# A contiguous copy by ScalarE ahead of the forward transform along d, with the planner's costs and order drawn anew

## The chip, the cores and the metric

One core of one Trainium2 chip runs the kernel. The metric is the device time of one execution in microseconds, the median of several runs.

## The reference

x is one sequence of S = 2048 tokens with D = 576 values each. Two branches read it and a gate per token mixes them.

```python
g = _sigmoid((x * gate_w).sum(-1, keepdims=True))
# branch a: a spectral filter over tokens and features
X = jnp.fft.rfft2(x, axes=(-2, -1)) * (w_r + 1j * w_i)
a = jnp.fft.irfft2(X, s=(S, D), axes=(-2, -1))
# branch b: 32 heads, each picks one of 64 x 64 = 4096 experts
q = jnp.einsum("nd,dhc->nhc", xf, w_q)            # 2 x 128 per head
s1 = jnp.einsum("nhd,ed->nhe", q[..., :128], k1)  # 64 scores
s2 = jnp.einsum("nhd,ed->nhe", q[..., 128:], k2)  # 64 scores
e = argmax(s1) * 64 + argmax(s2)
act = _gelu(jnp.einsum("nd,nhkd->nhk", xf, u[e]))
b = jnp.einsum("nhk,nhk,nhkd->nd", softmax(best, over 1), act, v[e])
return g * a + (1 - g) * b
```

All of it is float32. The two argmax lists decide which rows of u and v each token reads.

## The kernel before, in words

**Branch b, scores.** The 2048 tokens are 16 tiles of 128. The heads come in 8 chunks of 4; a chunk has 4 x 2 x 64 = 512 score columns. `build_m` multiplies the chunk's part of w_q with the keys (line 452, "build"), and ScalarE cuts the product into a high and a low part, mh and ml (lines 457 and 464). `scores` (line 472 on) takes a pair of token tiles and multiplies their x, also cut in two parts, with mh and ml: 14 matmuls of 128x512 for a tile and chunk, so 1792 in all. VectorE takes the maximum over each 64 columns (`mx`, line 502), ScalarE the sign of the distance to it (`sg`, line 510), and a few small steps make the index of the row (`ei`).

**Branch b, rows.** For each token tile and each head one gather (GpSimd, line 636 or 743) brings 128 rows of u and v side by side, 128 x 2 x 576 floats = 590 KB, into one of 12 buffers `uv` (13 in the late part). There are 512 gathers. VectorE forms the dot product with x (line 648, or 752 in the late part), ScalarE the gelu (line 652 or 755), and the factor `a` follows (line 657, 661 or 756). The v half is added up in one of three ways: by VectorE, by ScalarE and VectorE together, or by TensorE as a matmul with a diagonal matrix `dg` (made in line 702, used in line 706). The tiles 0 to 10 go through `group`. The tiles 11 to 15 go through `quad`, which works on four heads at once in quarters of the partitions; it needs x repeated four times (`xr`, line 733, 16 copies by ScalarE for each tile), a diagonal from VectorE (`dg`, line 758) and eight small matmuls (line 766).

**Branch a.** Its buffers take the place of those of the scores, so it begins when the last scores are done. `fold` (line 890 on) brings each of the 16 token tiles into the tile `BT` of 128 x 5 x 128 x 16 floats: partition, block of features, token group, and phase q of 16. `f2` (line 926) is the forward transform along d for one q: six matmuls (`along`, line 919), each recorded as two passes, that take `BT[:, i, :, q]` as the stationary operand, so 128 columns that lie 16 floats apart. `f4` (line 945), `f5` (line 965) and `f6` (line 975) transform along the tokens, multiply with the weights and go back; the result is written into the same slots of `BT`. `unit_front` calls `f2` for q = k and, but for k = 0 and 8, for q = 8 + k too, 16 calls in all. `invert` (line 1066 on) goes back along d: also `along`, with 128 columns of `BT` that lie side by side, and a second product (`go9`). The mix and the store follow.

**What sets the order.** Nothing is in a fixed order by hand. Every operation is a job with an engine, a duration, a due time and the buffers that it touches. `Plan.order` plays the jobs through: an engine that is free takes the ready job with the earliest due time that gets its buffers. Durations and latencies are numbers in the code (`REACH`, `LAND` and `HOP` in lines 101 to 103, and the second argument of each `plan`, `dv` and `ac`); due times are offsets (lines 1147 to 1192) plus a table `NUDGE` of some 900 entries. Each engine then runs its jobs in the order of that play, in order: an instruction that waits holds up those behind it.

Of the kernel before, what the change touches and what calls it, by code (L numbers as in the profile page):

```python
# [17 lines left out]
ALU = mybir.AluOpType  # L18
AX = mybir.AxisListType

P = 128
# [255 lines left out]
def tile_kernel(ctx, tc, xn, xT, x5, wqT, wq5, kT, wri, uv, gw, t_kr, t_ff, t_fv, t_tw, t_io, out):  # L277
# [162 lines left out]
    def build_m(c, i, at, after=()):  # L440
# [14 lines left out]
        plan("PE", 1.7, at, go, [pm], [wq, kTb], after=after)  # L455
# [16 lines left out]
    def scores(c, tp, at):  # L472
# [7 lines left out]
        def part(j, i):  # L480
# [12 lines left out]
            return plan("PE", 0.2275 * len(seq), at, go, [(ps, j)], list(use.values()))  # L493
# [13 lines left out]
        def signs(j, g0):  # L507
# [5 lines left out]
            plan("ACT", 0.784, at + O_SIGN, go, [sg], [(ps, j), (mv, tp)])  # L513
# [12 lines left out]
        dv(0.07 + 512 / 1920, at + O_MIN + nd("n", c, tp), lambda: vt(sq.ap[:, k], s2()[:, :, : E // 2], s2()[:, :, E // 2 :], ALU.min), [(sq, k)], [sg])  # L526
# [7 lines left out]
        dv(0.07 + n * 256 / 1920, at + O_MIN + nd("n", c, tp), lambda: vt(q2()[:, :, :Q], q2()[:, :, :Q], q2()[:, :, Q:], ALU.min), keys, [])  # L534
        dv(0.07 + n * 256 / 1920, at + O_MIN + nd("n", c, tp), lambda: vt(q2()[:, :, :Q], q2()[:, :, :Q], ramp.ap[:, :Q].unsqueeze(1).to_broadcast([P, n * 4 * HPC, Q]), ALU.add), keys, [ramp])
# [36 lines left out]
    def shuffle(src, dst, c0, c1, at, rd, wr):  # L572

        for q in range(HPC):
# [6 lines left out]
            plan("ACT", 4 * 0.2, at + O_TURN, go, wr, rd)  # L581
# [47 lines left out]
    def group(t, c, at, ahead, gate_by=(), ks=range(HPC), mixed=False):  # L629
# [22 lines left out]
        ac(0.1, at + O_GELU, lambda: actv(b.ap[:, k0:k1], z.ap[:, k0:k1], AF.Gelu_apprx_tanh), [b], zk, table="gelu")  # L652
# [47 lines left out]
        for k in range(0 if t in PAIR else HPC):  # L700
# [8 lines left out]
            plan("PE", 0.97, at + (O_D if t < NE else O_DL) + nd("p", t, c), go, [pd], [dg, (rows[k], 1)])  # L709
# [16 lines left out]
    def repeat(t, at, after):  # L726
# [4 lines left out]
        for j in range(HPC):  # L731
            for q in range(HPC):
                ac(act(576), at + 0.6 * j, lambda j=j, q=q: actv(  # L733
                    xr[t][j].ap[QB * q : QB * q + QB, :], x.ap[QB * j : QB * j + QB, :], AF.Copy), [(xr[t][j], q)], [x], after=after)

    def quad(t, c, at, ahead, gate_by, last):
# [18 lines left out]
        ac(0.1, at + O_QGELU, lambda: actv(b.ap, z.ap, AF.Gelu_apprx_tanh), [b], [(z, j) for j in range(HPC)], table="gelu")  # L755
# [14 lines left out]
        quads[t, c] = plan("PE", 1.25, at + O_QD + nd("p", t, c), go, [pd], [dg] + [(g, 1) for g in rows])  # L770
# [82 lines left out]
    for m, tag, pool, n in (  # L853
            (0, "bt", "la", 1), (0, "f5", "la", 2), (0, "kr", "la", 1), (0, "rp", "la", 1), (0, "eiq", "la", 1), (1, "lq", "lb", 1), (1, "krb", "lb", 1),
# [35 lines left out]
    def fold(t, at):  # L890
# [22 lines left out]
        plan("PE", 2.5, at, go, [pb], [(f, i) for i in range(5)] + [(kr, 0), (kr, 1), (kr, 2)])  # L913
# [31 lines left out]
    def f4(k2, X, at):  # L945
# [16 lines left out]
        plan("PE", 1.95, at, go, [p], [X, (tw, 0), (tw, 1)])  # L962
# [12 lines left out]
    def f6(k2, zb, tw, at):  # L975
# [16 lines left out]
        plan("PE", 2.39, at, go, [pt], [(zb, 0), (zb, 1), (tw, 0), (tw, 2), (tw, 3)])  # L992
# [26 lines left out]
    def unit_back(z, at):  # L1019
# [20 lines left out]
        dv(0.21, at, lambda: vt(BT.ap[:, 2, :, qc], ta.ap[:, 512:], pb.ap[:, 1, :P], ALU.add), [c_], src)  # L1040
        dv(0.21, at, lambda: vt(BT.ap[:64, 2, :, qs], pb.ap[64:, 1, :P], ta.ap[64:, 512:], ALU.subtract), [s_], src)
        dv(0.21, at, lambda: vt(BT.ap[64:, 2, :, qs], ta.ap[:64, 512:], pb.ap[:64, 1, :P], ALU.subtract), [s_], src)
# [23 lines left out]
    def invert(t, at):  # L1066
# [6 lines left out]
        plan("PE", 2.0, at, go, [p], [fv] + every)  # L1073
# [15 lines left out]
        plan("PE", 1.95, at + 3, go9, [p9], [(krb, 0), (krb, 1), (w, 0), (w, 1)])  # L1089
# [59 lines left out]
O_LESS = -173.264  # L1149
O_S0 = -1609.196  # L1150
A_ACT = True
A_OF = {0: (1, 6), 1: (3, 5, 6), 2: (0, 1, 2, 3, 4, 5, 6), 3: (0, 2, 4, 5, 6), 4: (0, 3, 4, 5, 6), 5: (0, 2, 5, 6, 7), 6: (0, 1, 5, 6), 7: (1, 2, 3, 4, 7), 8: (5, 6), 9: (0, 1, 4, 6, 7), 10: (1, 4, 7), 11: (0, 3, 4, 5, 6), 12: (0, 1, 4, 7), 13: (0, 1, 2, 6), 14: (0, 1, 2, 5, 7), 15: (0, 2, 5)}
O_SCALE = 232.282
# [239 lines left out]
```

## Time and profile before

| | us |
|---|---|
| median of 3 runs | 969.99 (968.39 to 970.98) |
| the profiled execution | 966.69 |
| its span, first to last instruction | 964.9 |
| TensorE busy / weight loads | 895.5 / 711.5 |
| VectorE busy | 835.1 |
| ScalarE busy | 642.9 |
| GpSimd busy | 556.4 |

1.8 us of the profiled execution lie around the span, and it is 3.3 us under the median. PE is TensorE's matmuls, PEld its weight loads, DVE VectorE, ACT ScalarE, POOL GpSimd, SP the queue of plain loads and stores. In the lists of instructions the columns are start, duration (both us), engine, line, operation, out<-in, the shape, and xN for N records; a bracket tells how long the engine stood idle before and who released it. Tile names stand without numbers: `p` is a PSUM tile, `fi` a transform table, `bt` the tile `BT`.

### The profile page before, as it was taken

What the parts mean: (1) busy time and instruction counts of PE and PEld (TensorE: products, weight loads), DVE (VectorE), ACT (ScalarE), POOL (GpSimd) and SP (SyncE); (2) the same over time, 40 slices, a digit from 0 to 9 for tenths busy, and PEclk for the clock granted to TensorE, in tenths of its full rate; (3) what the DMA queues carried; (4) which work ended last, traced back from release to release, by engine and by line L of the source; (5) the groups of instructions that cost most, each with busy time, mean ns of one, the idle gap of its engine ahead of it and who ended that gap; (6) DMA issues with size and microseconds to landing.
All of it is one profiled execution on the core that took longest, in us unless ns stands there. A gap on an engine that the chain in (4) does not pass through costs nothing.

```text
span 964.9 us, 16362 instructions
## 1 busy us (share of the span) xinstructions
PE 895.5 (93%) x5078; PEld 711.5 (74%) x5078; DVE 835.1 (87%) x2026; ACT 642.9 (67%) x2237; POOL 556.4 (58%) x516
## 2 busy tenths in 40 slices
PE   7899999967999999997999999959799999997998
PEld 6788888855888888876878787736467777765775
DVE  3679999989999999998999999859866899886876
ACT  3798977679777767577796989895642431615433
POOL 0227565746666665666656676637766556546661
PEclk9999999988999999998999999979999999998999
DMA  9769999988999999998999999999999999999996
GB/s 327 241 237 356 372 370 384 360 293 302 399 356 349 410 369 334 408 368 326 385 369 374 364 388 366 393 362 349 378 393 365 391 354 398 343 369 362 381 417 242
DMA packets 90902, 345.06 MB, mean 358 GB/s; under 512 B 10112, under 2 KB 10752, under 8 KB 90816
## 3 DMA queue, kind: packets, MB, share of 16 engines
q0 software_dynamic: 73728, 302.02, 82.4%
q1 hardware_dynamic: 17088, 42.01, 11.8%
q8 instruction: 40, 0.66, 0.3%
q14 instruction: 46, 0.38, 0.1%
HBM read 339.27 MB, written 4.72 MB: 356 GB/s over the span
## 4 chain that ended last, share of the span: by engine, by line
PE 53%; DVE 19%; ACT 11%; DMA 10%; issue 4%; POOL 1%; SPq 1%; DVEq 0%; ACTq 0%; POOLq 0%
PE p L346 53%; DVE uv L648 5%; DMA uv<-uv,ei 5%; ACT sg L510 3%; DVE xn L680 3%; ACT xr L733 3%; DVE xn L674 2%; DMA tw<-t_tw 2%; DVE uv L752 2%; DVE mx L502 2%; ACT uv L673 1%; POOL uv L636 1%; DMA xl<-xn 1%; DMA uv<-wqT 1%; DMA uv<-wq 1%
## 5 line engine op out<-in xcount | busy, mean ns | idle before, releaser
L636 POOL DMA_INDIRECT uv<-uv,ei x352 | 386.8, 1099 | 280.7 <-PE p L346 62.8
L648 DVE SCALAR_TENSOR_TENSOR uv<-uv,xn 128x576 f32<-128x576 f32 x352 | 260.4, 752 | 5.8 <-DMA uv<-uv,ei 5.7
L346 PE MATMUL p<-mh,xt 128*128 128x512 f32 x768 | 261.9, 399 | 0.8 <-DVE xn L718 0.8
L510 ACT ACTIVATE sg<-p,mx 128x64 bf16<-128x64 f32 x1024 | 235.1, 375 | 37.6 <-DVE mx L502 32.2
L743 POOL DMA_INDIRECT uv<-uv,eiq x160 | 169.4, 1059 | 108.8 <-PE p L346 55.1
L346 PE MATMUL p<-uv,dg 128*32 128x288 f32 (+1 forms) x1104 | 172.0, 423 | 36.4 <-DVE dg L758 15.9
L346 PE MATMUL p<-ml,xt 128*128 128x512 f32 x448 | 176.6, 394 | 0.0
L346 PEld LDWEIGHTS p<-uv,dg 128*32 128x32 f32 (+1 forms) x1104 | 107.8, 147 | 83.9 <-DVE dg L758 19.2
L346 PEld LDWEIGHTS p<-mh,xt 128*128 128x128 f32 x768 | 144.8, 189 | 33.4 <-DVE xn L718 1.3
L346 PE MATMUL p<-mhx,xt 128*128 128x512 f32 x384 | 136.4, 404 | 7.9 <-ACT sg L510 7.0
L752 DVE SCALAR_TENSOR_TENSOR uv<-uv,xr 128x576 f32<-128x576 f32 x160 | 116.7, 752 | 0.7 <-DMA uv<-uv,eiq 0.5
L346 PEld LDWEIGHTS p<-ml,xt 128*128 128x128 f32 x448 | 84.4, 188 | 17.7
L346 PE MATMUL p<-kT,uv 128*128 128x128 f32 x640 | 80.9, 283 | 15.2 <-ACT sg L510 6.2
L346 PEld LDWEIGHTS p<-kT,uv 128*128 128x128 f32 x640 | 79.3, 198 | 20.1 <-ACT sg L510 6.7
L346 PEld LDWEIGHTS p<-mhx,xt 128*128 128x128 f32 x384 | 73.2, 191 | 24.8 <-ACT sg L510 7.2
L680 DVE SCALAR_TENSOR_TENSOR xn<-uv,a,xn 128x576 f32<-128x576 f32 x111 | 89.6, 810 | 0.2
L674 DVE TENSOR_TENSOR xn<-uv,xn 128x576 f32<-128x576 f32 x114 | 86.0, 755 | 4.2 <-ACT uv L673 3.9
L502 DVE TENSOR_REDUCE mx<-p 128x16 f32<-128x1024 f32 x64 | 77.9, 1219 | 13.2 <-PE p L346 13.1
L673 ACT ACTIVATE uv<-uv,a 128x576 f32<-128x576 f32 x114 | 84.3, 813 | 5.2 <-DVE a L661 5.2
L521 ACT ACTIVATE sg<-sg 128x256 bf16<-128x256 bf16 x192 | 81.5, 470 | 0.7
L346 PE MATMUL p<-fi,bt 128*128 128x145 f32 (+3 forms) x384 | 80.3, 363 | 0.9 <-ACT t L1014 0.9
L346 PEld LDWEIGHTS p<-fi,bt 128*128 128x128 f32 x384 | 71.3, 248 | 8.8 <-issue 3.5
(117 smaller groups left out, 1080.7 us busy)
## 6 DMA issues: line engine op xcount, KB each, us to landing
uv<-wqT SPq DMA_DIRECT2D x32, 512.0 KB, 7.2
uv<-uv,ei POOLq DMA_INDIRECT x352, 6.9
w<-wri SPq DMA_DIRECT2D x16, 289.0 KB, 6.6
out<-xn SPq DMA_DIRECT2D x16, 288.0 KB, 5.9
xn<-xn SPq DMA_DIRECT2D x11, 288.0 KB, 6.1
uv<-uv,eiq POOLq DMA_INDIRECT x160, 7.1
tw<-t_tw SPq DMA_DIRECT2D x9, 256.0 KB, 6.9
uv<-xT SPq DMA_DIRECT2D x8, 256.0 KB, 7.2
```

The source lines that it names most:

```text
L346: after("PE", nc.tensor.matmul(*args, **kw))
L502: dv(dve(1024, True), at + O_MAX + nd("m", c, tp), lambda: nc.vector.tensor_reduce(mv.ap[:, 2 * tp : 2 * tp + 2, :], ps.ap.rearrange("p a ...
L510: on("ACT", actv(sg.ap[:, j, g, :], ps.ap[:, j, g * E : g * E + E], AF.Sign, bias=mv.ap[:, 2 * tp + j, g : g + 1], scale=-1.0))
L521: ac(act(256), at + O_ADD, lambda b=b: actv(s2()[:, :, b * Q : b * Q + Q], s2()[:, :, b * Q : b * Q + Q], AF.Copy, bias=b / 4), [sg], [])
L636: on("POOL", nc.gpsimd.indirect_dma_start(out=g.ap.rearrange("p a d -> p (a d)"), out_offset=None, in_=uv, in_offset=bass.IndirectOffsetOn ...
L648: dv(0.68, at + O_DOT + nd("d", t, c), lambda k=k, g=rows[k], xk=xk: stt(g.ap[:, 0, :], g.ap[:, 0, :], 1.0, xk.ap, op0=ALU.mult, op1=ALU.m ...
L673: ac(act_by(576), at + O_SCALE + nd("v", t, c), lambda v=v, s=s: actv(v(), v(), AF.Copy, scale=s()), [(rows[k], 1)], [a])
L674: dv(dve(576), at + O_SUM + nd("v", t, c), lambda v=v: vt(y.ap, v(), y.ap, ALU.add), [y], [(rows[k], 1)])
L680: dv(0.73, at + O_SUM + nd("v", t, c), lambda v=v, s=s: stt(y.ap, v(), s(), y.ap, op0=ALU.mult, op1=ALU.add), [y], [(rows[k], 1), a])
L733: ac(act(576), at + 0.6 * j, lambda j=j, q=q: actv(xr[t][j].ap[QB * q : QB * q + QB, :], x.ap[QB * j : QB * j + QB, :], AF.Copy), [(xr[t][ ...
L743: on("POOL", nc.gpsimd.indirect_dma_start(out=g.ap.rearrange("p a d -> p (a d)"), out_offset=None, in_=uv, in_offset=bass.IndirectOffsetOn ...
L752: dv(0.68, at + O_QDOT + nd("d", t, c), lambda j=j: stt(rows[j].ap[:, 0, :], rows[j].ap[:, 0, :], 1.0, xr[t][j].ap, op0=ALU.mult, op1=ALU. ...
```

## The change

`f2` gets one more step. ScalarE copies the 5 x 128 columns of one q into a contiguous tile `fl`, and the six matmuls read that. There is one such tile. The planner gets other durations and latencies, new offsets, and a new `NUDGE` table, so nearly every engine's order is another one. No other operation is added, taken away or given to another engine.

```diff
-REACH = {'POOL': 3.72, 'SP': 1.04}
+REACH = {'POOL': 2.7, 'SP': 1.04}
-HOP = {'PE': 0.36, 'DVE': 0.05, 'ACT': 0.32, 'POOL': 0.97, 'SP': 0.23}
+HOP = {'PE': 0.3, 'DVE': 0.12, 'ACT': 0.2, 'POOL': 0.6, 'SP': 0.23}
...
-            return plan("PE", 0.2275 * len(seq), at, go, [(ps, j)], list(use.values()))
+            return plan("PE", 0.236 * len(seq), at, go, [(ps, j)], list(use.values()))
...
-                ac(act(576), at + 0.6 * j, lambda j=j, q=q: actv(
+                ac(0.69, at + 0.6 * j, lambda j=j, q=q: actv(
...
+            (0, "bt", "la", 1), ..., (1, "fl", "lb", 1), (1, "lq", "lb", 1), (1, "krb", "lb", 1),
...
     def f2(q, at):
         p = psum()
-
-        def go():
-            along(p, ff, HO, lambda i: BT.ap[:, i, :, q])
-
-        plan("PE", 2.0, at, go, [p], [ff, (BT, "q", q)] + [(BT, "in", t, i) for t in range(NT) for i in range(3)])
+        flat = buf("fl", [P, ND, P])
+        ac(act(640), at + O_FLAT, lambda: actv(flat.ap, BT.ap[:, :, :, q], AF.Copy), [flat], [(BT, "q", q)] + [(BT, "in", t, i) for t in range(NT) for i in range(3)])
+        plan("PE", 2.0, at, lambda: along(p, ff, HO, lambda i: flat.ap[:, i, :]), [p], [ff, flat])
         return p
...
-        dv(0.21, at, lambda: vt(BT.ap[:, 2, :, qc], ta.ap[:, 512:], pb.ap[:, 1, :P], ALU.add), [c_], src)
+        dv(0.395, at, lambda: vt(BT.ap[:, 2, :, qc], ta.ap[:, 512:], pb.ap[:, 1, :P], ALU.add), [c_], src)
...
-ROWS = 1.5
+ROWS = 1.45
...
-    ('a', 0, 0): 4.95, ('a', 0, 1): -78.87, ('a', 0, 2): 294.57, ('a', 0, 3): 155.15, ('a', 0, 4): 38.86, ('a', 0, 5): -72.04,
...
```

The other durations move in the same manner: a build from 1.7 to 1.74, four signs from 0.784 to 0.81, an inverse transform from 2.0 to 2.06, `f4` from 1.95 to 2.1, a fold from 2.5 to 2.4, a quad's matmuls from 1.25 to 1.14.

**First place: TensorE in the forward transform along d.** Before, two transforms (PSUM tiles 1351 and 1365) stand next to each other and both read `bt`; the rows are the second half of one and the first half of the next.

```order
L346 MATMUL p2_1351_7986<-fi_1271_6732,bt_1269_6932 128x145
L346 MATMUL p2_1351_7986<-fi_1271_6732,bt_1269_6932 128x144
L346 MATMUL p2_1351_7986<-fi_1271_6732,bt_1269_6932 128x289
L346 MATMUL p2_1365_8009<-fi_1271_6732,bt_1269_6932 128x145
L346 MATMUL p2_1365_8009<-fi_1271_6732,bt_1269_6932 128x144
L346 MATMUL p2_1365_8009<-fi_1271_6732,bt_1269_6932 128x289
```

After the change two transforms still stand next to each other, and they read two copies, `fl` 7947 and 8026, that lie in the same buffer one after the other.

```order
L346 MATMUL p_1352_8010<-fi_6668,fl_7947 128x145
L346 MATMUL p_1352_8010<-fi_6668,fl_7947 128x144
L346 MATMUL p_1352_8010<-fi_6668,fl_7947 128x289
L346 MATMUL p_1355_8033<-fi_6668,fl_8026 128x145
L346 MATMUL p_1355_8033<-fi_6668,fl_8026 128x144
L346 MATMUL p_1355_8033<-fi_6668,fl_8026 128x289
```

The order of the two is unchanged; between them there is now a copy on another engine. Of the 16 transforms five follow the one ahead directly, as here; three more have one quad's eight small matmuls between, and the other seven have more.

**The same place on ScalarE, after the change.** Line 929 is the copy; `b` is a gelu of the quads (line 755), `t2` the transform's way out of PSUM, `dg` a diagonal.

```order
L929 ACTIVATE fl_1353_7947<-bt_1269_6762 128x640
L1011 ACTIVATE t2_1375_7950<-p2_1373_7917 128x289
L702 ACTIVATE dg_1141_7953<-ident_81,a_1136_7924 128x128
L1012 ACTIVATE t2_1375_7950<-p2_1373_7917 128x289
L755 ACTIVATE b_1624_7965<-z_1623_7908 128x4
L929 ACTIVATE fl_1356_8026<-bt_1269_6762 128x640
L755 ACTIVATE b_1632_8029<-z_1631_7976 128x4
L929 ACTIVATE fl_1389_8050<-bt_1269_6762 128x640
```

Each copy stands in ScalarE's queue behind the gelus and diagonals of the rows, and a gelu stands behind a copy that needs the buffer of the one ahead.

**Second place: ScalarE where the scores end and branch a begins.** The rows are the copies `xr` of the first late tile, and the way to a diagonal `dg` of an early tile. Before, from the end of the copies:

```order
L733 ACTIVATE xr_1523_6911<-xl_1275_6720 32x576 x4
L616 ACTIVATE lq_1_6756<-lq_1_6756 128x160
L510 ACTIVATE sg_1206_6750<-p2_1205_6583,mx_1061_5915 128x64 x4
L621 ACTIVATE lq_1_6756<-lq_1_6756 128x160
L915 ACTIVATE bt_1269_6932<-p2_1311_6705 128x2x128
L941 ACTIVATE tw_1331_6739<-tw_1331_6739 128x128
L942 ACTIVATE tw_1331_6739<-tw_1331_6739 128x2x128
L943 ACTIVATE tw_1331_6739<-tw_1331_6739 128x128
L652 ACTIVATE b_1262_6939<-z_1261_6836 128x4
L887 ACTIVATE krb_1273_6743<-krb_1273_6743 128x128
L521 ACTIVATE sg_1206_6750<-sg_1206_6750 128x16x16
L657 ACTIVATE a_1263_6943<-b_1262_6939,sw_1062_6542 128x1 x4
```

Behind these stand two more copies of `tw` and then `dg` 1265, the next diagonal that TensorE needs; ahead of them stand seven more `xr` copies in a row. After the change:

```order
L733 ACTIVATE xr_1536_6791<-xl_1275_6655 32x576 x2
L616 ACTIVATE lq_1_6700<-lq_1_6700 128x160
L733 ACTIVATE xr_1536_6791<-xl_1275_6655 32x576
L621 ACTIVATE lq_1_6700<-lq_1_6700 128x160
L733 ACTIVATE xr_1536_6791<-xl_1275_6655 32x576
L733 ACTIVATE xr_1537_6826<-xl_1275_6655 32x576 x4
L733 ACTIVATE xr_1538_6836<-xl_1275_6655 32x576 x3
L652 ACTIVATE b_1238_6846<-z_1237_6719 128x4
L733 ACTIVATE xr_1538_6836<-xl_1275_6655 32x576
L657 ACTIVATE a_1239_6851<-b_1238_6846,sw_1062_6404 128x1 x4
L733 ACTIVATE xr_1539_6857<-xl_1275_6655 32x576
L702 ACTIVATE dg_1241_6861<-ident_81,a_1239_6851 128x128
```

The whole row of sixteen `xr` copies has stretched out: the diagonal of the group that TensorE needs next (`dg` 1241) now follows thirteen of them and no `tw` copy. On TensorE two folds stand right ahead of that group; before, a fold and another group (`dg` 1138 to 1141) stood ahead of `dg` 1265.

More of the change, by code (lines that the diff above doesn't have):

```diff
@@ L768, in go @@
                        start=c == 0, stop=c == NCH - 1)
-        quads[t, c] = plan("PE", 1.25, at + O_QD + nd("p", t, c), go, [pd], [dg] + [(g, 1) for g in rows])
+        quads[t, c] = plan("PE", 1.14, at + O_QD + nd("p", t, c), go, [pd], [dg] + [(g, 1) for g in rows])
         if c < NCH - 1:
@@ L911, in go @@
                            start=n == 0, stop=n == 1)
-        plan("PE", 2.5, at, go, [pb], [(f, i) for i in range(5)] + [(kr, 0), (kr, 1), (kr, 2)])
+        plan("PE", 2.4, at, go, [pb], [(f, i) for i in range(5)] + [(kr, 0), (kr, 1), (kr, 2)])
         for r in range(2):
@@ L1184 @@
 TPS = 12.22
-AHEAD = -114.454
-TLAG = -61.614
+AHEAD = -283.177
+TLAG = 12.546
 FPACE = 1.418
```

61 lines of the change are left out of this document (31 added, 30 removed), and 293 rows, old and new, of the table NUDGE.

## The prediction

> **What bounds the kernel now.** I read the page's sums first, then its slices, then the chain that ended last, then every idle stretch of TensorE.
>
> ```profile
> span 964.9 us, 16362 instructions
> PE 895.5 (93%) x5078; PEld 711.5 (74%) x5078; DVE 835.1 (87%) x2026; ACT 642.9 (67%) x2237; POOL 556.4 (58%) x516
> PEclk9999999988999999998999999979999999998999
> DMA  9769999988999999998999999999999999999996
> GB/s 327 241 237 356 372 370 384 360 293 302 399 356 349 410 369 334 408 368 326 385 369 374 364 388 366 393 362 349 378 393 365 391 354 398 343 369 362 381 417 242
> DMA packets 90902, 345.06 MB, mean 358 GB/s; under 512 B 10112, under 2 KB 10752, under 8 KB 90816
> PE 53%; DVE 19%; ACT 11%; DMA 10%; issue 4%; POOL 1%; SPq 1%; DVEq 0%; ACTq 0%; POOLq 0%
> ```
>
> Three resources are nearly full: TensorE at 93%, VectorE at 87%, the DMA engines at nine tenths in most slices. The chain spends 53% of the span on TensorE. TensorE is idle for 964.9 - 895.5 = 69 us. Six stretches make more than half of it; each row below is the work that follows one, with the idle time in its bracket.
>
> ```profile
> 204.26 6.62 PE L346 MATMUL p<-uv,dg 128*128 128x288 f32 x16 [5.07 <-ACT sg L510]
> 222.61 0.80 PE L346 MATMUL p<-mhx,xt 128*128 128x512 f32 x1 [7.03 <-ACT sg L510]
> 447.00 3.78 PE L346 MATMUL p<-kT,uv 128*128 128x128 f32 x16 [6.24 <-ACT sg L510]
> 645.21 6.32 PE L346 MATMUL p<-uv,dg 128*128 128x288 f32 x16 [11.30 <-ACT dg L702]
> 700.62 2.15 PE L346 MATMUL p<-uv,dg 128*32 128x288 f32 x16 [6.15 <-DVE dg L758]
> 872.43 2.15 PE L346 MATMUL p<-uv,dg 128*32 128x288 f32 x16 [4.16 <-DVE dg L758]
> 232.37 4.15 PE L346 MATMUL p<-uv,dg 128*128 128x288 f32 x16 [0.32 <-ACT sg L510]
> ```
>
> Their sum is 39.95 us, 28.65 without the one at 645. The last row is the same group of sixteen as the first after a short wait: 4.15 us against 6.62, and 6.32 behind the stretch of 11.30. So the work behind a long stretch runs 2.2 to 2.5 us slower, say 2.3, and the digits of the granted clock dip in those slices. A long stall costs its idle time plus 2.3 us; the five without the one at 645 cost 28.65 + 5 x 2.3 = 40.2 us, or 8.0 us each.
>
> **The copy and the transforms.** The two users of `bt` as weights differ only in the step between columns; the first row is the stretch of f2, the second that of `invert`.
>
> ```profile
> L346 PEld LDWEIGHTS p<-fi,bt x192: 291/311/319, 724.5 to 850.1; 128*128 128x128 f32 x192
> L346 PEld LDWEIGHTS p<-fi,bt x175: 186/189/193, 883.8 to 953.1; 128*128 128x128 f32 x175
> 730.73 5.60 PE L346 MATMUL p<-fi,bt 128*128 128x145 f32 x24
> 895.67 4.20 PE L346 MATMUL p<-fi,bt 128*128 128x145 f32 x24
> 724.00:852.00 128.00, 125.08 (x867) 96.46 (x866) 107.46 (x275) 44.42 (x108) 72.69 (x71) 1.00 0.98 372
> ```
>
> The median load takes 311 ns with the step and 189 ns without. Two transforms in a row take 5.60 us with it, two of `invert` 4.20, so a contiguous stationary operand saves (5.60 - 4.20) / 2 = 0.70 us for each f2, **11.2 us** for 16. TensorE is busy for 125.08 of 128 us in that stretch, so this is time of the engine that sets the pace there.
>
> The copy costs ScalarE time and makes TensorE wait. No such copy is in the trace. These rows bound it: a write with the same step against one of runs of 16 side by side, and a plain copy.
>
> ```profile
> L915 ACT ACTIVATE bt<-p x32: 362/374/406, 641.5 to 721.2; 128x256 f32<-128x256 f32 x32
> L1025 ACT ACTIVATE bt<-p x4: 593/600/603, 743.9 to 879.4; 128x256 f32<-128x256 f32 x4
> L733 ACT ACTIVATE xr<-xl 32x576 f32<-32x576 f32 x80 | 54.4, 680 | 1.0
> 846.91 0.41 ACT L1013 ACTIVATE t<-p 128x289 f32<-128x289 f32 x1 [3.24 <-PE p L346]
> 847.22 0.41 ACT L1014 ACTIVATE t<-p 128x289 f32<-128x289 f32 x1
> 847.68 3.09 PE L346 MATMUL p<-fi,bt 128*128 128x145 f32 x12 [0.86 <-ACT t L1014]
> ```
>
> If the step costs ScalarE nothing, 640 elements take 0.680 x 640 / 576 = 0.76 us. If it costs what the weight load pays, (311 - 189) / 128 = 0.95 ns a column, they take 0.76 + 0.61 = 1.37 us; what the write pays is (600 - 374) / 256 = 0.88 ns, nearly the same. The load reads the very same addresses, so I take 1.3 us. ScalarE is busy for 44.42 of those 128 us, and 16 x 1.3 = 21 us find room; in time they aren't free. There is one tile `fl`, so a copy waits until the transform ahead has read it. Five times the next transform follows directly, and there TensorE stands still for the whole round trip. The last three rows show one: ScalarE's two copies last 847.63 - 846.91 = 0.72 us and TensorE's gap is 0.86, so a round trip is the copy plus 0.14 us. That gives 5 x 1.44 = 7.2 us. Three times a quad's matmuls lie between, 1.18 us (row below); they leave 0.3 us uncovered, 0.9 in all. The other seven have `f4`, `f6` or more between, over 2 us, and cost nothing; without that cover each would cost 1.4. In the copy's place 8.1 us come back, and the transforms bring **11.2 - 8.1 = 3.1 us**; with the fast copy (0.90 x 5 = 4.5 back) 6.7.
>
> ```profile
> 880.15 1.18 PE L346 MATMUL p<-uv,dg 128*32 128x288 f32 x16 [1.26 <-DVE dg L758]
> 632.65 7.60 ACT L733 ACTIVATE xr<-xl 32x576 f32<-32x576 f32 x11
> 626.31 2.46 PE L346 MATMUL p<-kr,f 128*128 128x256 f32 x24
> 640.27 0.34 ACT L616 ACTIVATE lq<-lq 128x160 f32<-128x160 f32 x1
> 641.30 0.35 ACT L621 ACTIVATE lq<-lq 128x160 f32<-128x160 f32 x1
> 642.49 0.22 ACT L652 ACTIVATE b<-z 128x4 f32<-128x4 f32 x1
> 643.10 0.85 ACT L657 ACTIVATE a<-b,sw 128x1 f32<-128x1 f32 x4
> 644.77 0.97 ACT L702 ACTIVATE dg<-ident,a 128x128 f32<-128x128 f32 x3
> ```
>
> The Trainium skill, "TensorE: Matmul & The Clock Gate", section "LDWEIGHTS (loading the stationary operand)", gives a weight load a time by its number of columns alone, whatever their step. By that rule f2 would save nothing and the round trips would be pure loss, the third rival below; the two rows of loads, 311 and 189 ns at equal columns, speak against it.
>
> **The place at 645 us.** TensorE waits 11.30 us for a diagonal that ScalarE makes at 644.77, behind eleven `xr` copies (7.60 us), signs and copies of `tw`. In the new order the next diagonal stands behind thirteen `xr` copies, 13 x 0.68 = 8.8 us, and the four small steps of the rows, 0.34 + 0.35 + 0.22 + 0.85 = 1.8 us, from the first copy on; on TensorE two folds of 2.46 us cover 4.9 us of that. What is left is 5.7 us, if the copies begin when the first fold does. So **5.6 us** go. It is still long enough for the slow stretch behind it. VectorE's dots end late there too, which bounds the gain: the stall can also stay whole, or go whole (0 to 11.3).
>
> **The rest of the order.** No engine gets other work, so only waits can change. One row shows that the new durations come nearer to what is recorded: a bt addition is planned at 0.395 us instead of 0.21, and an `xr` copy at 0.69 instead of 0.56 where its row above has 0.680.
>
> ```profile
> L1040 DVE TENSOR_TENSOR bt<-f,p x7: 355/374/375, 765.1 to 868.0; 128x128 f32<-128x128 f32 x7
> DVE uv L648 <- DMA uv<-uv,ei: 5.7, 10, 1.1
> DMA to landing us min/median/max: 4.5/6.9/14.3
> POOL uv L636 <- PE p L346: 62.8, 46, 9.9
> POOL uv L743 <- PE p L346: 55.1, 37, 6.2
> ```
>
> An order laid by better numbers meets fewer surprises, but it is a new order of the same crowded engines and brings stalls of its own. How many of the other five long stalls go isn't in any row: none to five of them bound it on the good side, some more of them on the bad side. I take one net, **8.0 us**, by judgement.
>
> The sum is 3.1 + 5.6 + 8.0 = 16.7 us. Against the profiled execution of 966.69 that is 950.0; it was 3.3 us under the median of 969.99, so I predict **953.3**.
>
> **Rivals.**
>
> More stalls go. If three of the five go, the sum is 3.1 + 5.6 + 24.0 = 32.7 and the time 937.3. For it: PE's 69 idle us and the slow work behind them are the largest loss in the profile. Against it: VectorE and DMA are nearly full as well.
>
> Nothing changes, because the stream of rows is the limit. It moves the same 345.06 MB, and its share is 0.98 in the transforms' stretch. What TensorE saves would come back as waiting for rows, and the time stays 970.0. Against it: seven slices reach 393 to 417 GB/s, at 400 the bytes need 863 us, and GpSimd waits 62.8 + 55.1 us for matmuls to free its buffers, so an earlier matmul also starts a gather earlier. The Trainium skill, "SBUF — State Buffer", section "A bandwidth-pool intuition that's wrong (but worth ruling out)", gives one core about 358 GB/s from HBM, the very mean of the page; by that figure the bytes alone would need an estimated 964 us and this rival would be sure. The slices at 384 to 417 speak against it as a limit here.
>
> The load isn't faster. If the 311 ns come from something other than the step, say from what else runs in that stretch, f2 saves nothing, the round trips stay, and the sum is 8.1 - 5.6 - 8.0 = -5.5: 964.5. Against it: all 192 loads lie between 291 and 319 ns, all 175 others between 186 and 193, with no overlap.
>
> Slower: VectorE waits for rows. The planner's latency of a gather on idle DMA engines, from GpSimd's start to VectorE's, was 1.45 + 3.72 + 1.5 + 0.2 + 0.97 = 7.84 us and becomes 1.45 + 2.7 + 1.45 + 0.2 + 0.6 = 6.40 (the 1.45 of GpSimd and the 0.2 of LAND stay). Landings take 6.9 us in the median. With 7.84 VectorE waited for rows only 5.7 us in the whole span; with 6.40 the plan adds its own queueing to a smaller base, and more dots come up before their rows. VectorE is in order, so the maxima and factors behind such a dot wait too, and with them the signs, the PSUM tiles and TensorE. The price is 8.0 us for each wait that grows long. The 8.7 us of the first two terms are used up by 1.1 more long stalls than before; with three more it is 24.0 - 8.7 = 15.3 us slower, 985.3. Against it: 4.5 us is the shortest landing, so 6.40 isn't too short for a queue that is empty.
>
> **How the numbers follow.** The forecast has a chance of 0.42 (its own range 942 to 965), three stalls gone 0.13, the slow load 0.07, no change 0.10, slower 0.28. Below 967.1 lie the first three: faster by over 0.3% (about what a measurement of this kernel can tell from no change) 0.62; within it 0.10; slower 0.28. The range reaches from below the second case to above the last, 931 to 988; some 0.06 lies under it and 0.10 over it.
>
> **What would show it.** Right: the weight loads from `fl` take about 189 ns; a transform of twelve records about 2.1 us; sixteen copies about 1.3 us each; idle times of TensorE of about 1.4 us before the direct followers, released by the copy; some 5.7 us idle where the scores end; five slow stretches of the clock, not six; PE busy about 11 us less. Wrong: copies of 0.8 us or above 1.5; loads of 311 ns; VectorE waiting for rows by tens of us instead of 5.7; idle times over 4 us at new places.

## The result, and the profile after

The changed kernel takes 973.9 us (median of 20 runs, 970.2 to 976.8) against 967.1 us of the kernel before beside it (20 runs, 965.0 to 971.0). The ratio is 1.0064, with an interval of 1.0050 to 1.0077: 0.6% slower, where 953.3 us, 1.4% faster, was forecast. The profiled execution took 975.08 us.

The page of the changed kernel, the lines that answer to those of before:

```profile
span 973.3 us, 16358 instructions
PE 892.2 (92%) x5078; PEld 697.0 (72%) x5078; DVE 838.9 (86%) x2026; ACT 663.2 (68%) x2253; POOL 567.6 (58%) x516
PEclk9999999999999999999999999979899999998999
DMA  9959989798899998899999999999999999999997
GB/s 328 298 204 360 388 304 386 251 333 313 314 384 354 370 384 323 305 379 356 326 343 382 347 349 347 394 367 361 411 393 410 394 368 410 363 391 378 392 417 304
DMA packets 90902, 345.06 MB, mean 355 GB/s; under 512 B 10112, under 2 KB 10752, under 8 KB 90816
DMA 27%; PE 24%; DVE 21%; issue 12%; POOL 7%; ACT 7%; SPq 0%; POOLq 0%; DVEq 0%; ACTq 0%
```

TensorE has 3.3 us less work (892.2 against 895.5) and 12 us more idle time (973.3 - 892.2 = 81.1 against 69.4). The chain that ended last runs through other engines: TensorE had 53% of it and has 24%, the transfers had 10% and have 27%. The rates show some of the places where transfers were missing: slices 8, 16 and 17 are at 251, 323 and 305 GB/s, where before they were at 360, 334 and 408.

The span in three stretches, cut at the first matmul of the forward transform along d and at the first of the inverse one, first of the kernel before, then of the changed one. The columns are the length, then busy time (and instructions) of PE, PEld, DVE, ACT and POOL, the granted clock, the DMA share and GB/s.

```profile
0.00:724.80 724.80, 669.41 (x3447) 541.15 (x3448) 641.55 (x1523) 555.77 (x2007) 427.13 (x391) 0.97 0.95 356
724.80:881.30 156.50, 147.28 (x1058) 109.65 (x1057) 131.25 (x338) 49.58 (x123) 87.56 (x86) 0.98 0.97 369
881.30:964.90 83.60, 78.81 (x580) 60.65 (x576) 62.31 (x166) 37.55 (x108) 41.76 (x39) 0.99 0.89 349
```

```profile
0.00:732.00 732.00, 673.04 (x3431) 539.78 (x3432) 635.76 (x1501) 552.28 (x1994) 428.13 (x383) 0.98 0.93 345
732.00:888.00 156.00, 138.95 (x1057) 96.15 (x1055) 139.03 (x356) 71.83 (x150) 93.74 (x91) 0.98 1.01 390
888.00:973.30 85.30, 80.24 (x596) 61.05 (x592) 64.15 (x170) 39.13 (x110) 45.75 (x43) 1.00 0.94 367
```

Of the 8.4 us by which the span grew, 7.2 lie ahead of the first forward transform, where one copy of the 16 has run. In the middle stretch TensorE is busy for 8.3 us less (138.95 against 147.28), and the stretch is as long as before: the gain is there, and it has turned into idle time. The DMA share has gone the other way: lower in the first stretch (0.93 against 0.95), higher in the two others (1.01 and 0.94 against 0.97 and 0.89), since nine more of GpSimd's gathers are left when the first stretch ends (91 + 43 against 86 + 39).

The new steps of the changed kernel, its weight loads, its copies, one transform that directly follows another, and the waits that belong to the copy (in us: total, times, longest):

```profile
L346 PEld LDWEIGHTS p<-fi,fl x192: 186/189/193, 731.7 to 860.9; 128*128 128x128 f32 x192
L929 ACT ACTIVATE fl<-bt x16: 1283/1314/1341, 725.4 to 858.0; 128x640 f32<-128x640 f32 x16
760.09 2.23 PE L346 MATMUL p<-fi,fl 128*128 128x145 f32 x12 [1.41 <-ACT fl L929]
PE p L346 <- ACT fl L929: 8.2, 8, 1.5
ACT fl L929 <- PE p L346: 30.6, 14, 7.1
```

The loads take 189 ns, the copies 1.31 us, a transform 2.23 us where it took 2.8, and TensorE waits 8.2 us for copies, eight times. All of that is close to the forecast (189 ns, 1.3 us, 2.1 us, 8.1 us). TensorE's busy time isn't: it was to fall by about 11 us and fell by 3.3, with 3.6 us more ahead of the transforms. The last row isn't in the forecast either: ScalarE stood 30.6 us at copies whose tile `fl` was still being read, and what was behind them in its queue stood too.

TensorE's longest idle times in the changed kernel, after its start:

```profile
229.47 0.79 PE L346 MATMUL p<-mhx,xt 128*128 128x512 f32 x1 [4.55 <-ACT sg L510]
650.23 6.78 PE L346 MATMUL p<-uv,dg 128*128 128x288 f32 x16 [8.77 <-ACT dg L702]
703.41 6.92 PE L346 MATMUL p<-uv,dg 128*128 128x288 f32 x32 [5.54 <-ACT dg L702]
881.63 4.76 PE L346 MATMUL p<-tw,t 128*128 128x256 f32 x24 [2.53 <-DVE t L969]
```

Where there were six of 4.2 to 11.3 us there are three of 4.6 to 8.8, and the digits of the granted clock dip in three slices instead of five. So long stalls did go, and yet TensorE is idle for longer: by many short waits. What grew is this, waits of the changed kernel (the first was 5.7 us in 10 times before):

```profile
DVE uv L648 <- DMA uv<-uv,ei: 47.2, 69, 2.1
DVE uv L752 <- DMA uv<-uv,eiq: 20.2, 34, 1.2
POOL uv L636 <- DVE xn L680: 53.5, 28, 14.8
L636 POOL DMA_INDIRECT uv<-uv,ei x352: 933/1070/2494, 37.1 to 745.6; - x176
DMA to landing us min/median/max: 4.3/6.9/16.1
```

VectorE meets its rows late 103 times, 67 us in all, none of them longer than 2.1 us, and GpSimd waits 53.5 us for buffers that VectorE's sums free late. Of the kernel before, the same wait of GpSimd:

```profile
POOL uv L636 <- DVE xn L680: 10.7, 13, 1.9
```

The median landing of the 352 early gathers is 6.9 us as before; the longest is 16.1 instead of 14.3. That of the 160 late gathers rises from 7.1 to 8.4 us.

### The profile page after: what moved, and what is told of

Same layout as the page of the kernel before. It is cut to its first block, busy times and chain, and to the rows that moved or that the text cites. A ratio compares the mean times of both kernels' runs of the same rounds, so it can differ in the third digit from the quotient of the medians.

```text
span 973.3 us, 16358 instructions
## 1 busy us (share of the span) xinstructions
PE 892.2 (92%) x5078; PEld 697.0 (72%) x5078; DVE 838.9 (86%) x2026; ACT 663.2 (68%) x2253; POOL 567.6 (58%) x516
## 3 DMA queue, kind: packets, MB, share of 16 engines
q0 software_dynamic: 73728, 302.02, 82.2%
q1 hardware_dynamic: 17088, 42.01, 11.8%
## 4 chain that ended last, share of the span: by engine, by line
DMA 27%; PE 24%; DVE 21%; issue 12%; POOL 7%; ACT 7%; SPq 0%; POOLq 0%; DVEq 0%; ACTq 0%
PE p L346 24%; DMA uv<-uv,ei 19%; POOL uv L636 6%; DVE uv L648 6%; DMA uv<-uv,eiq 5%; DVE xn L680 3%; DVE xn L674 3%; ACT sg L510 2%; DVE mx L502 2%; DMA xl<-xn 2%; ACT fl L929 1%; POOL uv L743 1%; DVE sq L526 1%; DVE uv L752 1%; ACT xr L733 1%
## 5 line engine op out<-in xcount | busy, mean ns | idle before, releaser
L636 POOL DMA_INDIRECT uv<-uv,ei x352 | 399.3, 1134 | 294.8 <-issue 55.9
L510 ACT ACTIVATE sg<-p,mx 128x64 bf16<-128x64 f32 x1024 | 231.7, 361 | 32.6 <-DVE sq L526 16.2
L346 PE MATMUL p<-kT,uv 128*128 128x128 f32 x640 | 84.1, 290 | 13.4 <-ACT kT L786 5.1
L346 PEld LDWEIGHTS p<-kT,uv 128*128 128x128 f32 x640 | 82.1, 205 | 18.4 <-ACT sg L510 5.4
L521 ACT ACTIVATE sg<-sg 128x256 bf16<-128x256 bf16 x192 | 79.3, 453 | 0.5
L346 PE MATMUL p<-mlx,xt 128*128 128x512 f32 x192 | 76.7, 399 | 0.0
L652 ACT ACTIVATE b<-z 128x4 f32<-128x4 f32 x88 | 19.8, 225 | 74.2 <-DVE uv L648 73.8
```

The costliest lines, as they stand in the source:

```text
L346: after("PE", nc.tensor.matmul(*args, **kw))
L510: on("ACT", actv(sg.ap[:, j, g, :], ps.ap[:, j, g * E : g * E + E], AF.Sign, bias=mv.ap[:, 2 * tp + j, g : g + 1], scale=-1.0))
L521: ac(act(256), at + O_ADD, lambda b=b: actv(s2()[:, :, b * Q : b * Q + Q], s2()[:, :, b * Q : b * Q + Q], AF.Copy, bias=b / 4), [sg], [])
L636: on("POOL", nc.gpsimd.indirect_dma_start(out=g.ap.rearrange("p a d -> p (a d)"), out_offset=None, in_=uv, in_offset=bass.IndirectOffsetOn ...
L652: ac(0.14, at + O_GELU, lambda: actv(b.ap[:, k0:k1], z.ap[:, k0:k1], AF.Gelu_apprx_tanh), [b], zk, table="gelu")
```

## The experiments

All ratios are to the kernel before on the same chip. The chips weren't alike: on those of the runs below the kernel before took 1011.6 us (the first four runs), 1011.8 (the four beside each other), 1002.6 (half of each late row), 1001.5 (contiguous weights and lighter products) and 966.6 (half of every row). The changed kernel stands at 1.0064 on the chip of the result and at 1.0058 on one where the kernel before takes 1011.8, so this ratio carried over where the times didn't; a ratio set beside one from another chip is marked below.

**The order without the copy, the copy without the order.** Theory 1 was that the new order loses and the copy pays, theory 2 the reverse. In the first kernel the copy stays a job of the planner, which keeps every engine's order, and emits nothing:

```diff
-        ac(act(640), at + O_FLAT, lambda: actv(flat.ap, BT.ap[:, :, :, q], AF.Copy), [flat], ...)
-        plan("PE", 2.0, at, lambda: along(p, ff, HO, lambda i: flat.ap[:, i, :]), [p], [ff, flat])
+        plan("ACT", act(640), at + O_FLAT, lambda: None, [flat], ...)
+        plan("PE", 2.0, at, lambda: along(p, ff, HO, lambda i: BT.ap[:, i, :, q]), [p], [ff, flat])
```

> The changed kernel's order of instructions on every engine, without its 16 copies: the forward transform reads its weights again in steps of 16 floats, so that of the change the new order alone is left. Theory 1 (the new order loses, the copy pays): the net of the copy in the changed kernel was -11.2 us of TensorE against 8.2 us of TensorE's waits for it, -3 us, so this kernel comes out slower still, 973 to 980 us where the kernel before has 967, a ratio of 1.007 to 1.013; the loads of the 192 weights go back to 311 ns, and the first of these matmuls starts near 732 us as in the changed kernel. Theory 2 (the copies lose, by the 30.6 us in which ScalarE's queue stood at them and by TensorE's waits): this kernel is at the kernel before or below, 960 to 968 us, ratio 0.993 to 1.001.

Measured 0.9997 (0.9956 to 1.0039): inside theory 2's range, outside theory 1's. The second kernel puts the copies into the finished order of the kernel before:

```diff
     def f2(q, at):
-            along(p, ff, HO, lambda i: BT.ap[:, i, :, q])
+            along(p, ff, HO, lambda i: fl[i])
...
+    for n, j in enumerate(f2s):
+        low = max([at_[d] for d, _ in j.deps] + ([at_[f2s[n - FL]]] if n >= FL else [])) + 1
+        soon = next(x for x, d in enumerate(done) if d.start >= j.start - FLEAD)
+        turn.setdefault(min(max(low, soon), at_[j]), []).append((n, j))
...
+FL, FLEAD = 1, 3.0
```

> The order of the kernel before on every engine, row for row, with the 16 copies put into ScalarE's queue (up to 3 us of planned time ahead of their matmuls, into one tile as in the changed kernel): of the change the copy alone is left. Theory 1 (the new order loses, the copy pays): TensorE gains 16 x 0.70 = 11.2 us, and waits about 1.44 us in each of 4 places where one of these transforms stands right behind another (5.8 us) and some 0.3 us in others (1 to 2 us); together -4, so 961 to 965 us against 967 of the kernel before, ratio 0.994 to 0.998. Theory 2 (the copies lose): 972 to 978 us, ratio 1.005 to 1.011, as the changed kernel.

Measured 0.9970 (0.9929 to 1.0010): theory 1's number, though the interval reaches 1. Its waits for copies:

```profile
PE p L346 <- ACT fl L1149: 4.7, 4, 1.5
ACT fl L1149 <- PE p L346: 15.1, 5, 5.1
```

TensorE waits 4.7 us in four places, where 5.8 were expected, and ScalarE stands at copies in this order too.

With two tiles in turn every other copy goes into tiles that the scores have left. One number is changed against the run above; the lines behind it, which were there already, now run for every other copy:

```diff
-FL, FLEAD = 1, 3.0
+FL, FLEAD = 2, 3.0
...
             x = pools["gp"].tile([P, 4, P], F32, tag="sg.0", bufs=1, name=f"fla_{n}")
             y = pools["gp"].tile([P, P], F32, tag="mx.0", bufs=1, name=f"flb_{n}")
             on("ACT", actv(x, BT.ap[:, :4, :, q], AF.Copy))
             on("ACT", actv(y, BT.ap[:, 4, :, q], AF.Copy))
```

> The same with two tiles for the copies in turn (the second one in tiles that the scores have left, so that every other copy is two instructions), so that a copy needn't wait for the transform just ahead of its own. Theory 1 (the copy pays and only its round trips cost): the 4 x 1.44 us go, and ScalarE no longer stands at a copy; -11.2 + 1 to 3 us, 956 to 960 us, ratio 0.989 to 0.993, faster than both kernels. Theory 2 (the copies lose by ScalarE's time, 16 x 1.31 = 21 us, whatever the tiles): at or above the kernel before, 967 us or more.

Measured 0.9878 (0.9845 to 0.9912), just under theory 1's range. The second tile is worth 0.9%: that is what waiting for the one tile cost. The same two tiles in the changed kernel's order, where the tile is chosen when the copy's job is emitted:

```diff
-        ac(act(640), at + O_FLAT, lambda: actv(flat.ap, BT.ap[:, :, :, q], AF.Copy), [flat], ...)
+        flat.make = make
+        plan("ACT", act(640), at + O_FLAT, copy, [flat], ...)
...
+            count[0] += 1
+            if count[0] % 2:
+                x = one(g, slot)
```

> The changed kernel's order with two tiles for the copies in turn. Theory 1 (the order's loss lies ahead of the transforms): the 8.2 us of TensorE's waits for copies go to 1 to 3, and the time falls by 4 to 7 us to 967 to 970 us, ratio 1.000 to 1.004; the first transform along d still starts near 732 us, 7 us late. Theory 2 (ScalarE's queue standing 30.6 us at the copies is what loses): well under the kernel before, 958 to 964 us, ratio 0.991 to 0.997.

Measured 0.9972 (0.9928 to 1.0016), between the two: theory 1 has 1.000 to 1.004, theory 2 0.991 to 0.997, and the interval reaches into both.

**Four kernels beside each other.** The first is the changed kernel itself; the others are the first three from above, so no diff is new.

> The changed kernel itself, beside the kernel before on one chip, since in the first four runs the kernel before took 1011.6 us where it had taken 967. Both theories: if this chip is as the first one, a ratio of 1.005 to 1.008. Theory 1 (the new order loses where rows come late) would have it slower on a chip with slow transfers too; theory 2 (the copies lose) has it slower by as much on either chip.

Measured 1.0058 (1.0022 to 1.0095).

> The changed kernel's order without its copies, once more, beside the changed kernel on one chip. Theory 1 (order loses, copy pays 3 us): a ratio to the kernel before of 1.007 to 1.013, above that of the changed kernel by 0.003. Theory 2 (copies lose): 0.993 to 1.001. After the first look (0.9997, 0.996 to 1.004, on a slower chip) theory 2 is ahead here.

Measured 1.0001 (0.9973 to 1.0029).

> The order before with the copies in one tile, once more. Theory 1 (order loses, copy pays): 0.994 to 0.998. Theory 2 (copies lose): 1.005 to 1.011. After the first look (0.997, 0.993 to 1.001) theory 1 is ahead here; with the run above, a third theory is that the two cost little apart and lose together, where the new order leaves ScalarE less room for the copies: then this one and the run above are both within 0.997 to 1.001, and only the changed kernel is at 1.006.

Measured 0.9971 (0.9940 to 1.0002).

> The order before with the copies in two tiles, once more. Theories 1 and 3: 956 to 960 us where the kernel before has 967, ratio 0.988 to 0.993 as in the first look (0.988). Theory 2 (the copies lose by ScalarE's time): 1.000 or more.

Measured 0.9883 (0.9850 to 0.9917). So the third theory holds as a description: the new order alone changes nothing, the copy alone pays 0.3% in one tile (not clear of noise by itself, but the same on two chips) and 1.2% in two, and both together lose 0.6%. In the new order the copy costs 1.0058 / 1.0001 = 0.6% where in the order before it pays 0.3%. Theories 1 and 2 both fall.

**Half of each late row.** Is it the stream of late rows that hides TensorE's gain in the new order?

```diff
-                    out=g.ap.rearrange("p a d -> p (a d)"), out_offset=None, in_=uv,
+                    out=g.ap[:, 0, :], out_offset=None, in_=uv.rearrange("n (a d) -> (n a) d", a=2),
...
-                    mm(..., rows[j].ap[:, 1, r * 288 : r * 288 + 288], ...)
+                    mm(..., rows[j].ap[:, 0, r * 288 : r * 288 + 288], ...)
```

> The kernel before with the 160 gathers of its late groups (those of eiq, which run beside the transforms) fetching 128 x 576 floats instead of 128 x 1152: they take 2304 bytes from half as far into the table, and the sums are made from the same 576 floats, so the output isn't the reference's. The 352 early gathers stay whole. It is the base of the next three; the order on every engine is that before. Theory 4 (in the new order the row stream, which has fallen behind by the scores' end, sets the time beside the transforms, and TensorE's 11 us there don't count; in the order before TensorE sets it): little gain here, 0 to 1.5%, ratio 0.985 to 1.000. Theory 1b (the new order costs by TensorE's own stalls): the same.

> The new order without copies, late gathers by half as in the run above. Theory 4: the new order is level with the order before where nothing is copied, so within 0.5% of the run above. Theory 1b: the same; the next two tell them apart.

> The order before with copies in two tiles, late gathers by half. Both theories: the copy pays as it does with whole rows, 1.2% (ratio to the kernel of the first of these four 0.988, plus or minus 0.004).

> The new order with copies in two tiles, late gathers by half. With whole rows the copies paid 0.3% in the new order (0.9972 against 1.000) and 1.2% in the order before (0.988). Theory 4 (the late row stream hides TensorE's gain in the new order): with the stream made lighter the copies pay 1.0 to 1.2% here too, and this kernel is within 0.4% of the run above. Theory 1b (the new order's own stalls on TensorE cost it 0.9% where copies are in ScalarE's queue): it stays 0.7 to 1.1% above the run above, and 0.2 to 0.4% below the second of these four.

Measured in this order 0.9953 (0.9924 to 0.9982), 0.9967 (0.9932 to 1.0002), 0.9863 (0.9824 to 0.9902) and 0.9960 (0.9929 to 0.9990). In the order before the copies pay 0.9863 / 0.9953, 0.9%; in the new order 0.9960 / 0.9967, nothing. The new order with copies stays 0.9960 / 0.9863 = 1.0% above the order before, as theory 1b has it. Theory 4 falls: the bytes of the late rows alone don't hide the gain.

**Contiguous weights without a copy.** The forward transform reads contiguous columns of the table it multiplies with, in both orders:

```diff
-            along(p, ff, HO, lambda i: BT.ap[:, i, :, q])
+            along(p, ff, HO, lambda i: ff.ap[:, i % 4, :P])
```

> The order before, no copies, and the 16 forward transforms take their weights in contiguous columns from the table that they multiply with, instead of from the tile bt: the same 192 loads and matmuls of the same shapes, wrong numbers, TensorE's gain without a copy and without a wait for one. Theories 5 and 6 alike: TensorE's 16 x 0.70 = 11.2 us come out, ratio 0.986 to 0.990.

> The same in the new order (no copies, weights in contiguous columns from the table, wrong numbers). Theory 5 (in the new order VectorE, with 9 more rows' work left when the transforms begin, sets the time beside them, and TensorE's gain doesn't count): no gain over the new order without copies, ratio 0.997 to 1.002. Theory 6 (the copies themselves, 16 x 1.3 us in ScalarE's queue, cost in the new order what TensorE gains): the gain comes out whole here, ratio 0.986 to 0.991.

Measured 0.9875 (0.9843 to 0.9907) and 0.9997 (0.9965 to 1.0030). The 192 loads of the first of the two, by tile:

```profile
L346 PEld LDWEIGHTS p<-fi x192: 186/190/193, 749.2 to 875.0; 128*128 128x128 f32 x192
```

This is the sharpest pair. The same 11 us taken from TensorE, with no copy anywhere, are worth 1.25% in the order before, all of them, and nothing in the new order, where the order alone stands at 1.0001 and 0.9997. So theory 6 (ScalarE's time for the copies) falls: in the new order the kernel's time doesn't follow TensorE's work in the transforms, even without copies. Two things limit this. The new order alone was run on other chips only. And in the profiled executions the stretch from the first forward to the first inverse transform is 166.2 and 166.4 us long in the new order alone and 159.3 here, so the gain may be there and be given back outside of that stretch.

**Less work for VectorE in the late part.**

```diff
-                rows[j].ap[:, 0, :], rows[j].ap[:, 0, :], 1.0, xr[t][j].ap, op0=...
+                rows[j].ap[:, 0, :288], rows[j].ap[:, 0, :288], 1.0, xr[t][j].ap[:, :288], op0=...
```

> The order before with copies in two tiles, and the 160 products of VectorE for the late rows over 288 columns instead of 576 (half of each product is left out): about 160 x 0.3 us less work for VectorE beside and behind the transforms, with everything else as it was. Base of the next run. Both theories: 0 to 1.5% faster than with whole products (0.988), ratio 0.973 to 0.988.

> The new order with copies in two tiles, and the late rows' products over 288 columns as in the run above. Theory 5 (VectorE sets the time beside the transforms in the new order): the 0.9% by which the new order stood above the order before, both with copies in two tiles, goes: within 0.4% of the run above. Theory 6 (the copies' time on ScalarE): it stays 0.7 to 1.1% above the run above.

Measured 0.9911 (0.9880 to 0.9941) and 1.0064 (1.0034 to 1.0093). The distance is 1.5%, not less. Theory 5 falls, and the 0.7 to 1.1% of theory 6 isn't met either. The 160 products take 0.45 us instead of 0.75 each, and VectorE is busy for 46 to 48 us less, yet neither kernel got faster by it, where 0 to 1.5% was expected: with whole products they stand at 0.988 and 0.997, on other chips. Why isn't known.

**Half of every row.** Now the early gathers too: the diff of the late ones, the same in line 636, and the sums on the half that is fetched. Order before and new order, both with copies in two tiles:

```diff
-                v = lambda k=k: rows[k].ap[:, 1, :]
+                v = lambda k=k: rows[k].ap[:, 0, :]
...
-                    mm(pd.ap[:, r, :288], dg.ap, rows[k].ap[:, 1, r * 288 : r * 288 + 288],
+                    mm(pd.ap[:, r, :288], dg.ap, rows[k].ap[:, 0, r * 288 : r * 288 + 288],
```

> The order before with copies in two tiles, and all 512 gathers by half (2304 bytes a row, the early ones too; all sums are made from the one half that is fetched, so the output isn't the reference's). Base of the next run. Theory 7 (the new order costs ahead of the transforms, where VectorE meets its rows late) and theory 8 (it costs by the order of work between the engines, whatever the rows' transfer takes) alike: 0.5 to 3% faster than with whole rows (0.988), ratio 0.96 to 0.985; the waits of VectorE for early rows stay under 10 us.

> The new order with copies in two tiles, all gathers by half. Theory 7: the waits for early rows (36 us with whole rows in this order) fall under 15 us, and the distance to the run above falls from 0.9 to 1.5% (as with whole rows, half late rows and light products) to under 0.5%. Theory 8: the distance stays at 0.9% or more, even where the waits for rows go.

Measured 0.9888 (0.9865 to 0.9911) and 0.9554 (0.9529 to 0.9579): 955.8 and 923.3 us where the kernel before takes 966.6. The stretches of the first, then of the second:

```profile
0.00:725.60 725.60, 673.19 (x3446) 545.49 (x3447) 640.28 (x1523) 557.31 (x2010) 426.73 (x391) 0.97 0.67 200
725.60:873.40 147.80, 135.27 (x1057) 94.13 (x1056) 130.60 (x338) 66.64 (x144) 87.67 (x87) 0.98 0.72 217
873.40:957.20 83.80, 78.85 (x580) 60.73 (x576) 62.31 (x166) 37.54 (x108) 41.83 (x40) 0.98 0.66 202
```

```profile
0.00:694.40 694.40, 662.13 (x3431) 535.24 (x3432) 629.48 (x1501) 552.09 (x1996) 429.88 (x383) 0.99 0.69 205
694.40:838.50 144.10, 135.40 (x1058) 94.69 (x1056) 134.91 (x347) 70.44 (x154) 93.50 (x91) 1.00 0.76 231
838.50:923.90 85.40, 80.31 (x596) 61.12 (x592) 66.45 (x179) 39.29 (x112) 47.90 (x44) 0.99 0.69 213
```

With light rows the new order begins its transforms at 694.4 us, 31 us ahead of the order before; that is 31 of the 33 us between the two spans. No more than one or two of the 16 copies have run by then, so this stretch can be set beside the kernel before and the changed kernel with whole rows, on a chip where the kernel before takes 967.1 us: there it was 724.8 in the order before and 732.0 in the new one. Half rows shorten it by 37.6 us in the new order and not at all in the order before. TensorE is idle for 923.9 - 877.8 = 46 us of the span, against 957.2 - 887.3 = 70, and its busy time is 9.5 us shorter too, at a granted clock of 0.99 against 0.97 in the first stretch. The landings of the early gathers and the waits for them, in the new order with half rows:

```profile
PE 877.8 (95%) x5078; PEld 691.1 (75%) x5078; DVE 830.8 (90%) x2026; ACT 661.8 (72%) x2261; POOL 571.3 (62%) x516
DMA to landing us min/median/max: 3.4/4.0/7.2
DVE uv L648 <- DMA uv<-uv,ei: 6.7, 9, 1.6
```

The same wait in the new order with two tiles and whole rows, on a slower chip:

```profile
DVE uv L648 <- DMA uv<-uv,ei: 35.8, 48, 2.2
```

And in the order before with half rows, where no wait of VectorE for an early row is left at all:

```profile
PE 887.3 (93%) x5078; PEld 700.3 (73%) x5078; DVE 833.2 (87%) x2026; ACT 661.5 (69%) x2261; POOL 556.2 (58%) x516
DMA to landing us min/median/max: 3.4/4.1/8.1
```

The early rows land in 4.0 or 4.1 us in both, instead of 6.9. GpSimd's wait for VectorE's sums, 53.5 us in the changed kernel, is still 34.9 with half rows, so most of it belongs to the order and not to late rows. The order before gains nothing by half rows, where both theories expected 0.96 to 0.985 (0.989 against 0.988 with whole rows on other chips, both with two tiles); the new order gains 4.2% (0.955 against 0.997, the two taken on different chips). Theory 7 holds in its direction and is far too small in size: it expected the distance between the orders to shrink to under 0.5%, and the new order came out 0.9554 / 0.9888, 3.4%, ahead. Theory 8 falls: it isn't the order of work as such. What the new order loses with whole rows goes with the transfers of the early rows, since half late rows alone left the distance between the orders as it was.

## Why the prediction was wrong

**The loads, right.** 11.2 us were to come from contiguous weights. The loads take 189 ns, and in the order before the contiguous weights alone are worth 1.25%, 12 us. The Trainium skill, "TensorE: Matmul & The Clock Gate", section "LDWEIGHTS (loading the stationary operand)", goes by the number of columns alone; by that rule the run with contiguous weights and no copy would have been level, and the measurement decides: 189 or 190 against 311 ns at equal columns.

**The copy's waits, right; its net, right by luck.** 8.1 us were forecast and 8.2 measured. The net of -3.1 us is what the copy brings in the order before (0.997), but there TensorE waits only 4.7 us for copies, and by the same sum 6.5 us would have come. The copy costs more than TensorE's waits for it: the blocked ScalarE (30.6 us) wasn't in the sum, and one tile instead of two costs 0.9% in the order before and as much in the new one (1.0058 against 0.9972, on different chips).

**The place where the scores end, mis-sized.** 5.7 us were to be left of 11.30, and 8.77 are, so 2.5 us went instead of 5.6.

**The rest of the order, wrong: this is the step that failed.** "I take one net, 8.0 us, by judgement." It was to bring 8.0 us, and 13.6 with the term above it. The new order alone measures 1.0001 (0.9973 to 1.0029), so it brings nothing, give or take 3 us. The stalls that the step spoke of did go; five were there beside the one at 645, and two are left of such a length. The step let them go at no price but a few other stalls. The price comes with the rows: with half rows, which land in 4.0 us, the new order is 3.4% faster than the order before, both with copies in two tiles; with whole rows, which land in 6.9 us in the kernel before and the changed one, all of that is taken back, and the new order is 0.9% slower (0.9972 against 0.9878). The nearest cause in the plan is its latency of a gather, 6.40 us from GpSimd's start to VectorE's against 7.84 in the order before, which has the slack; that number wasn't changed by itself, so this link is argued.

**The sum, wrong too.** It counted the transforms' terms in the new order as "time of the engine that sets the pace there". That was read off the profile of before, and it held for the order before only: the contiguous weights without a copy bring 0.0% in the new one. And the copy's net there isn't -3.1 us: the changed kernel over its order alone is 1.0058 / 1.0001, 0.57% of 967, +5.5 us, with some 4 us of noise either way. The two errors, 13.6 and 8.6 us, make up 22.2 of the 22.9 us between -16.7 us and the +6.2 us of the ratio, a closer fit than that noise lets one expect.

**The slower rival had the cause and not its form.** It named VectorE's waits for rows and the two latencies that bring them about, and its sign is that of the result. Its price was 8.0 us for each wait that grows long, 985 us in all. None of VectorE's waits grew long: 103 short ones, 67 us in all, stand in the place of 11 waits with 6 us, and the run with half rows shows that gains of the new order were hidden under what the rows cost. The rival of no change, the stream of rows as the limit, had the size (970) for the like reason. Beside it the prediction quoted the Trainium skill, "SBUF — State Buffer", section "A bandwidth-pool intuition that's wrong (but worth ruling out)", with about 358 GB/s for one core; the changed kernel too has slices at 410 to 417, so 358 isn't a limit in those slices.

**What stays open.** Half a row halves the bytes and shortens the landing at once, so late landings and full DMA engines (82.2% and 11.8% of the span for the two queues of rows and loads) aren't told apart. The traces of the chips where the kernel before takes over 1000 us hold no landing times, so the 6.9 us stand for the chip of the result alone. It isn't shown either by which path the early rows take away the gain in the stretch of the transforms, where half late rows alone don't give it back; that ScalarE's stand at the copies delays the rows' small steps behind them is only argued.

**A version that beats both.** The order before with copies in two tiles is at 0.988 on both chips where it ran, 1.2% faster than the kernel before, and 0.9883 / 1.0058, 1.7%, faster than the changed one beside it.

## What to carry to other kernels

An order that is better where data land early can be no better where they land late: price a new order by the waits of the engine that reads the data, and not only by the stalls that it removes elsewhere. A planner's latency for a transfer may be where such slack is given away, which was argued here and not shown. A gain on the engine that sets the pace is worth its time only in the order in which it sets the pace, so before two edits are added up, run each alone. A copy that runs ahead of its reader wants two tiles: the second was worth 0.9% here.

## What the runs showed of the hardware

- Weights of 128 fp32 columns that lie 64 bytes apart load in 311 ns, side by side in 189; a ScalarE copy of 128x640 from the same places takes 1.31 us.
- 46 to 48 us less work for VectorE made no kernel faster: with products over 288 instead of 576 columns the order before stood at 0.991 instead of 0.988 and the new one at 1.006 instead of 0.997, both with two tiles (on different chips).
- One and the same kernel took 966.6 to 1011.8 us on the chips of these runs.
- An early gather of 128 rows lands 4.0 or 4.1 us after its start in the median with 2304 bytes a row and 6.9 us with 4608, beside each kernel's other transfers.
